# A recurrent attention block and its feed-forward part on one core: feed-forward groups of three chunks instead of two

## The chip, the cores and the metric

The kernel runs on 1 core of one Trainium2 chip. The metric is the device time of one execution in microseconds; three runs of the kernel before gave 1131.92, 1136.14 and 1138.54 us, median 1136.14 us. The profile is of one more execution.

## The reference, cut to what matters

```python
# r, k, v, w, a, b: (B=4, H=8, S=768, D=40) float32
for t in range(S):
    y[:, :, t] = np.einsum('bhd,bhde->bhe', rt, state)
    Sa = np.einsum('bhde,bhe->bhd', state, at)
    state = state * wt[:, :, None, :] - np.einsum('bhd,bhe->bhde', Sa, bt)
    state = state + np.einsum('bhd,bhe->bhde', vt, kt)
x = y.transpose(0, 2, 1, 3).reshape(3072, 320)     # tokens x (heads * D)
h = np.maximum(x @ w_in, 0.0)                       # w_in: 320 x 2048
out = (h * h) @ w_out                               # w_out: 2048 x 320
```

The two weight matrices arrive as float64, and the kernel rounds them to float32 itself.

## The kernel before, in words

**Chunks and slots.** The sequence is cut into chunks of 128 tokens; 6 chunks in each of 4 batches make 24 chunks, in the order of `order` (batch fastest). The main loop at the end (L766) has one slot for each chunk. A slot has `TOTAL` = 12 steps. In every step `weave` gives each of several generators its share of turns, so the order of the instructions on every engine is written out by this interleaving and each engine then runs its own list in order:

- `chain(i)`: the sequential part of chunk i on the matmul engine (PE): the product of A with v, two triangular solves with T (tiles `xr`, `minus_x`), the state's growth, and the outputs into `tokens` (L615).
- `rest(i+1)`: preparation of the next chunk: transposes (L315, `turn`), the masked products A and RV (L331), and at its end the loads of T and N (`inverses`).
- `prepare(i+...)`: the decays of later chunks (scans L354 and L355, reciprocals L358 and L359) in slots 0 to 15.
- `second`, the generator `ffn()`: the feed-forward part. A group is `GB` chunks. For each of the 16 tiles of 128 hidden units it does the first layer (contraction over 320 = two full tiles of rows with `w_in` and one of 64 rows with `w_third`), then relu on ScalarE (ACT, L642) and a multiplication on VectorE (DVE, L643), which squares; then it yields. Two tiles are started together, and the two `w_third` products of such a pair use the two halves of the array's rows. Then the second layer adds up 16 products of 320 columns for each chunk, with a yield after every 4.
- `rounded`, the generator `rounding()`: float64 weights to float32 in 26 pieces (10 of 512 columns for `w_in` and `w_third`, then 16 of 320 columns for `w_out`), each with two ACT and five DVE instructions (L257, L261, L265, L266, L274 to L276), through two tiles of `ps_f`.

**Queues.** Nearly all transfers are issued by SyncE (SP), in program order, each issue waiting for what it depends on. `store` puts a transfer into `line`, and a later `tick` issues it. When the last chunk of a group has its tokens, eight transfers (`moves`, from L620) gather rows of `tokens` into the 64-row tile and the spare rows; the first layer of the group waits for them, and `gathered` says when the generator may emit it. GpSimd (POOL) inverts triangular blocks in `solve`, after `take` has fetched them; after slots 0, 1, 3, 5, 9, 13 and 15 `flush`, `take` and `solve` stand between two slots.

**Where the feed-forward part stands.** Slots 0 to 3 contain none of it; they round 4, 7, 8 and 8 pieces. Before slot 4 the loop runs 8 feed-forward turns alone (`before` in L768 to L771). In slots 4 to 23 it has 12 turns a slot, one in every step. What is left runs after the last slot (`run(second)`). A group has 24 turns. All but the last group have two PSUM tiles (`ps_f`), the last has four (`ps_w`).

**Memory.** `hidden` holds 17 tiles of 256 columns, used in rotation; before the feed-forward part begins, float64 weights land in its first part and in two tiles `raw0` and `raw1`, five places for `w_out` in turn (`in_turn`), and its end serves as scratch for the first chunks (`spare`).

L87 is the line of the helper `mm`, so all products have that line; tiles tell them apart: `ps_c` belongs to the chain, `ps_w` to the preparation, `ps_f` to the feed-forward part and the rounding. Each product of float32 leaves two records in the trace (704 records of 352 products), each transpose one.

Of the kernel before, what the change touches and what calls it, by code (L numbers as in the profile page):

```python
# [17 lines left out]
def kernel(  # L18
# [25 lines left out]
    DM = H * D  # L44
# [7 lines left out]
    NF = DFF // 128  # L52
    GB = 2

# [34 lines left out]
    def single(name, shape):  # L89
        return const.tile(shape, FP32, tag=name, name=name)  # L90
# [141 lines left out]
    WIDE = len(fetches)  # L232
    in_turn = [*own_, *lent]
    for f in range(NF):
        fetchable(in_turn[f % 5], [(0, 128, moe_w_out[f * 128:(f + 1) * 128, :])], [w_out[:, f, :]])
# [101 lines left out]


    def spare(name, i):
        n = ("mv", "turned", "joins").index(name)  # L340
        t_ = hidden[:, NF - 2 * n - i % 2] if i <= B else own_[n // 2][:, n % 2 * H * Q:(n % 2 + 1) * H * Q]
        return t_.rearrange("p (h t) -> p h t", h=H)

# [148 lines left out]
    def rest(i, g):  # L492
# [16 lines left out]
        yield  # L509
        g["A"] = masked("A", 4, kT, aT)  # L510
        yield
# [115 lines left out]
    def ffn():  # L627
        for gi in range(len(order) // GB):
# [4 lines left out]
            for f in range(0, NF, 2):  # L633
# [4 lines left out]
                for e, p_ in enumerate(ps):  # L638
                    for j in range(NT):
                        mm(p_, w_in[:, j, (f + e) * 128:(f + e + 1) * 128], t_[:, j, :], False)  # L640
                    h_ = hidden[:, (gi * NF + f + e) % (NF + 1)]
                    nc.scalar.activation(h_, p_, Act.Relu)  # L642
                    nc.vector.tensor_tensor(h_, p_, h_, Alu.mult)  # L643
                    hid.append(h_)
                    yield True
            while left():
                yield False
            for n in range(GB):
                bb, c = order[gi * GB + n]
                p_ = psum(ps_f if gi < len(order) // GB - 1 else ps_w)[:, :DM]  # L650
                for f in range(NF):
                    mm(p_, hid[f][:, n * C:(n + 1) * C], w_out[:, f], f == 0)
                    if f % PART == PART - 1 and f < NF - 1:
                        yield True
                o_ = new("o", [128, DM], 1)
                nc.scalar.copy(o_, p_)
# [7 lines left out]
    gathered = set()  # L664
    STEPS = NF + 4 * GB

# [91 lines left out]

    TOTAL = STEPS // GB
    ahead = {0: (4, 5), 1: (6, 7), 2: (8,), 3: (9,), 4: (10, 11), 5: (12, 13)}  # L760
    ahead.update({i: (i + 8,) for i in range(6, len(order) - 8)})
    share = {**{i: (0, 0) for i in range(B)}, B: (TOTAL, 8)}
    pieces_in = {0: 4, 1: 7, 2: 8, 3: 8}
    done = set(range(B))
    unit = unit_of[B]
    for i in range(len(order)):  # L766
        bb, c = order[i]
        n, before = share.get(i, (TOTAL, 0))  # L768
        for _ in range(before):
            next(second)  # L770
            tick()  # L771
        tc.no_sync_barrier()
# [52 lines left out]
```

## Time and profile before

| what | value |
|---|---|
| median of the three runs | 1136.14 us |
| the profiled execution, its own time | 1136.86 us |
| its span, first to last instruction | 1135.1 us |
| mean granted TensorE clock | 0.908 |
| PE busy | 1029.9 us (91%) |
| DVE busy | 482.1 us (42%) |
| ACT busy | 246.2 us (22%) |
| POOL busy | 651.7 us (57%) |
| DMA | 113.48 MB, mean 100 GB/s |

1.8 us of the profiled execution lie outside its span. A row of the timeline gives the start in us, the duration in us, the engine, the line, the operation, the tiles, how many records were merged, and in brackets how long the engine sat idle before and what released it. PEld is the loading of the stationary operand.

### The profile page before, as it was taken

The numbers are of one execution on the slowest core, as the hardware profiler recorded it, in microseconds if no ns is written. First come the engines' busy times: TensorE is split into PE (matmuls) and PEld (weight loads), VectorE is DVE, ScalarE is ACT, GpSimd is POOL, SyncE is SP. The second block draws the span as 40 slices with busy tenths as digits, with TensorE's granted clock in tenths as the row PEclk, the third lists the DMA queues.
The fourth block names the chain that finished last, engine by engine and source line by source line (L and its number), as shares of the span: only waits on it lengthen the run. The fifth ranks groups of instructions, "written<-read, shape, count | busy, mean of one in ns | idle before, by whom it ended". The sixth has DMA issues, their size and how long they took to land.

```text
span 1135.1 us, 19336 instructions
## 1 busy us (share of the span) xinstructions
PE 1029.9 (91%) x7632; PEld 811.9 (72%) x7632; DVE 482.1 (42%) x1004; ACT 246.2 (22%) x547; POOL 651.7 (57%) x1129
## 2 busy tenths in 40 slices
PE   6385787799999999999999999999999999999998
PEld 5375676668777777777777777777777777777666
DVE  6367877727355155154264253353143133330211
ACT  2123233222221122122112122113021121221111
POOL 5886628877874999603999802999858810000000
PEclk8666656689999999999989999999998999999999
DMA  9889977583648505519515518414243342030000
GB/s 116 154 151 210 182 177 178 124 154 77 135 106 156 121 36 109 152 39 167 116 48 101 123 65 150 118 49 84 58 117 69 77 90 58 10 83 12 7 12 12
DMA packets 262370, 113.48 MB, mean 100 GB/s; under 512 B 244168, under 2 KB 250440, under 8 KB 260616
## 3 DMA queue, kind: packets, MB, share of 16 engines
q1 hardware_dynamic: 257944, 93.24, 40.2%
q0 software_dynamic: 3248, 18.88, 7.0%
q8 instruction: 60, 0.98, 0.4%
q10 hardware_dynamic: 1088, 0.13, 0.2%
q14 instruction: 30, 0.25, 0.1%
HBM read 75.77 MB, written 34.48 MB: 97 GB/s over the span
## 4 chain that ended last, share of the span: by engine, by line
PE 69%; DVE 11%; DMA 10%; SPq 3%; POOL 2%; issue 2%; ACT 2%; DVEq 0%; POOLq 0%; ACTq 0%
PE ps_f L87 34%; PE ps_c L87 19%; PE ps_w L87 11%; PE ps_w L315 3%; DMA in_v<-in_v_dram 3%; DVE decay L358 1%; DVE decay L359 1%; PE ps_w L533 1%; SPq L108 1%; DMA in_r<-in_r_dram 1%; DMA blocks<-kept_t 1%; POOL half_t L435 1%; POOL half_p L433 1%; DMA in_w<-in_w_dram 1%; PE ps_c L543 1%
## 5 line engine op out<-in xcount | busy, mean ns | idle before, releaser
L433 POOL TENSOR_TENSOR half_p<-half_n,half_t 128x70 f32<-128x70 f32 (+52 forms) x502 | 288.5, 575 | 104.9 <-DMA half_n<-kept_d 55.4
L435 POOL TENSOR_TENSOR half_t<-half_t,half_p 128x70 f32<-128x70 f32 (+52 forms) x502 | 315.2, 628 | 39.3
L643 DVE TENSOR_TENSOR hid<-ps_f,hid 128x256 f32<-128x256 f32 x176 | 73.9, 420 | 350.3 <-ACT hid L642 349.9
L87 PE MATMUL ps_f<-w_out,hid 128*128 128x320 f32 x704 | 208.2, 444 | 0.1
L87 PE MATMUL ps_f<-tokens,w_in 128*128 128x256 f32 x704 | 199.5, 410 | 0.0
L87 PEld LDWEIGHTS ps_f<-w_out,hid 128*128 128x128 f32 x704 | 130.4, 193 | 49.5 <-issue 2.4
L87 PEld LDWEIGHTS ps_f<-tokens,w_in 128*128 128x128 f32 x704 | 124.6, 196 | 43.5 <-issue 30.3
L642 ACT ACTIVATE hid<-ps_f 128x256 f32<-128x256 f32 x176 | 67.4, 383 | 269.1 <-PE ps_f L87 268.6
L87 PE MATMUL ps_f<-tokens,w_third 64*128 64x256 f32 x352 | 86.0, 425 | 8.1 <-DVE hid L643 6.0
L87 PEld LDWEIGHTS ps_c<-xr,T 64*64 64x64 f32 x768 | 54.9, 150 | 23.6 <-issue 13.8
L87 PE MATMUL ps_c<-xr,T 64*64 64x40 f32 x768 | 60.7, 241 | 7.2 <-DMA T<-kept_t 2.4
L410 POOL DMA_DIRECT2D half_n<-kept_d x18 | 8.9, 501 | 98.0 <-DMA kept_d<-N 92.9
L87 PEld LDWEIGHTS ps_f<-tokens,w_third 64*128 64x128 f32 x352 | 40.0, 190 | 34.9 <-DVE hid L643 23.0
L354 DVE TENSOR_TENSOR_SCAN decay<-ps_w,ones 128x64 f32<-128x64 f32 x88 | 23.6, 268 | 85.1 <-PE ps_w L315 85.1
L87 PEld LDWEIGHTS ps_c<-in_v,A 128*128 128x128 f32 x384 | 51.2, 209 | 2.3
L87 PE MATMUL ps_c<-in_v,A 128*128 128x40 f32 x384 | 50.2, 294 | 0.0
L87 PE MATMUL ps_w<-rT,xnT 40*128 40x128 f32 x384 | 36.4, 309 | 12.6 <-DVE RV L331 12.1
L87 PEld LDWEIGHTS ps_w<-rT,xnT 40*128 40x128 f32 x384 | 29.9, 206 | 22.9 <-DVE RV L331 18.9
L615 DVE TENSOR_TENSOR tokens<-ps_c,dec 128x512 f32<-128x512 f32 x24 | 16.5, 688 | 66.1 <-PE ps_c L87 66.1
L545 ACT COPY sd<-ps_c 128x512 f32<-128x512 f32 x20 | 11.7, 586 | 144.8 <-PE ps_c L543 144.8
L87 PE MATMUL ps_w<-decay,bT 40*128 40x128 f32 x352 | 28.4, 307 | 14.6 <-DVE decay L363 14.6
L370 ACT COPY N<-ps_w 128x512 f32<-128x512 f32 x48 | 25.8, 589 | 63.8 <-PE ps_w L87 44.2
(148 smaller groups left out, 1441.8 us busy)
## 6 DMA issues: line engine op xcount, KB each, us to landing
kept_e<-decay SPq DMA_DIRECT2D x22, 780.0 KB
dec<-kept_e SPq DMA_DIRECT2D x22, 780.0 KB
half_n<-kept_d POOLq DMA_DIRECT2D x12, 384.0 KB, 9.4
half_n<-kept_d POOLq DMA_DIRECT2D x6, 768.0 KB, 11.5
in_w<-in_w_dram SPq DMA_DIRECT2D x24, 160.0 KB
in_ab<-in_b_dram SPq DMA_DIRECT2D x24, 160.0 KB
in_ab<-in_a_dram SPq DMA_DIRECT2D x24, 160.0 KB
in_k<-in_k_dram SPq DMA_DIRECT2D x24, 160.0 KB
```

The costliest lines, as they stand in the source:

```text
L87: nc.tensor.matmul(o, l_, r_, start=start, stop=True, skip_group_check=True)
L108: later(lambda: queue.dma_start(out=out_, in_=in_), steps)
L315: nc.tensor.transpose(p_[:, q * 128:(q + 1) * 128], pair(x_, q), ident)
L354: nc.vector.tensor_tensor_scan(up[:, q, MID + 1:C + 1], wT[:, q, MID:], ones, 1.0, Alu.mult, Alu.mult)
L358: nc.vector.reciprocal(down[:, :, MID + 1:C + 1], up[:, :, MID + 1:C + 1])
L370: nc.scalar.copy(t_[:, e * NP:(e + 1) * NP], p_)
L433: nc.gpsimd.tensor_tensor(p_, part[:, at:at + m_].unsqueeze(1).to_broadcast([128, n, m_]), t3[:, :n, s:s + 1].to_broadcast([128, n, m_]), ...
L435: nc.gpsimd.tensor_tensor(t3[:, :n, s + 1:], t3[:, :n, s + 1:], p_, Alu.subtract)
L545: nc.scalar.copy(sd.rearrange("p q e d -> p q (e d)"), quads(p_))
L615: nc.vector.tensor_tensor(t_, y_, g["up"][:, :, :C], Alu.mult)
L642: nc.scalar.activation(h_, p_, Act.Relu)
L643: nc.vector.tensor_tensor(h_, p_, h_, Alu.mult)
```

## The change

`GB` becomes 3: a group is three chunks, the first layer's products have 384 columns instead of 256, there are 8 groups instead of 12, and a group has 28 turns. In slot 4 the feed-forward part has 8 turns from step 4 on, in slots 5 to 23 it has 10 turns in 12 steps (none in steps 0 and 6); the 8 turns alone before slot 4 are gone. The pieces rounded in slots 0 to 4 are 4, 6, 6, 7 and 4 (the last four within the first four steps of slot 4). `hidden` has 16 tiles of 384 columns without rotation; the tiles `raw0` and `raw1` are gone, and `w_out` has seven places in `hidden` instead of five. A has two tiles instead of four, `in_r` and `minus_x` one each instead of two, the output tile `o` two instead of one.

```diff
-    GB = 2
+    GB = 3
...
-            rings[nm] = Ring(f"in_{nm}", 2, [128, H, DP], 0.0, pads)
+            rings[nm] = Ring(f"in_{nm}", 1 if nm == "r" else 2, [128, H, DP], 0.0, pads)
...
-    minus_x = Ring("minus_x", 2, [128, H, DP], 0.0, pads)
+    minus_x = Ring("minus_x", 1, [128, H, DP], 0.0, pads)
...
-    hidden = single("hid", [128, NF + 1, GB * C])
+    hidden = single("hid", [128, NF, GB * C])
...
-    lent = [free_words[:, 2 * DM * i:2 * DM * (i + 1)] for i in range(3)]
-    own_ = [single(f"raw{i}", [128, 2 * DM]) for i in range(2)]
+    in_turn = [free_words[:, at:at + 2 * DM] for at in [4 * WI + 2 * DM * i for i in range(4)] + [2 * DM * i for i in range(3)]]
+    LENT = len(in_turn)
...
-    then = {0: (WIDE,), 1: (3,), 2: (WIDE + 1,), 3: (4,), 5: (WIDE + 2, WIDE + 3), 6: (WIDE + 4,)}
-    then.update({NARROW + f: (WIDE + f + 5,) for f in range(NF - 5)})
+    then = {1: (3,), 2: (WIDE,), 3: (4,), 4: (WIDE + 1,), 5: (WIDE + 2,), 6: (WIDE + 3,), 7: (WIDE + 4,), 8: (WIDE + 5,),
+            9: (WIDE + 6,)}
+    then.update({NARROW + f: (WIDE + f + LENT,) for f in range(NF - LENT)})
...
-        g["A"] = masked("A", 4, kT, aT)
+        g["A"] = masked("A", 2, kT, aT)
...
-                    h_ = hidden[:, (gi * NF + f + e) % (NF + 1)]
+                    h_ = hidden[:, f + e]
...
-                o_ = new("o", [128, DM], 1)
+                o_ = new("o", [128, DM], 2)
...
-    TOTAL = STEPS // GB
+    TOTAL = 12
...
-    share = {**{i: (0, 0) for i in range(B)}, B: (TOTAL, 8)}
-    pieces_in = {0: 4, 1: 7, 2: 8, 3: 8}
+    share = {**{i: (0, 0) for i in range(B)}, B: (8, 4)}
+    pieces_in = {0: (4, TOTAL), 1: (6, TOTAL), 2: (6, TOTAL), 3: (7, TOTAL), B: (4, 4)}
...
-        n, before = share.get(i, (TOTAL, 0))
-        for _ in range(before):
-            next(second)
-            tick()
+        n, begin = share.get(i, (10, 0))
...
-        jobs.append((some(second, n), n, 0, TOTAL))
+        jobs.append((some(second, n), n, begin, TOTAL))
         if i in pieces_in:
-            jobs.append((some(rounded, 2 * pieces_in[i]), 2 * pieces_in[i], 0, TOTAL))
+            m_, end = pieces_in[i]
+            jobs.append((some(rounded, 2 * m_), 2 * m_, 0, end))
```

How this moves instructions is seen at three places. A row below is a run of like instructions on one engine, with the line, the operation, the tiles, the size and the count.

The first place is PE at the border of slots 3 and 4; `blocks,hid` is the last product of `rest(4)`, and `in_v,A` the first of `chain(4)`. Before:

```order
L87 MATMUL ps_w<-hid 32x32 x16
L87 MATMUL ps_w<-decay_131,bT 128x128 x8
L87 MATMUL ps_w<-blocks,hid 32x32 x16
L87 MATMUL ps_f<-tokens,w_third 128x256 x2
L87 MATMUL ps_f<-tokens,w_in 128x256 x4
L87 MATMUL ps_f<-tokens,w_third 128x256 x2
L87 MATMUL ps_f<-tokens,w_in 128x256 x4
```

The same place after the change:

```order
L87 MATMUL ps_w<-hid 32x32 x16
L87 MATMUL ps_w<-decay_129,bT 128x128 x8
L87 MATMUL ps_w<-blocks,hid 32x32 x16
L87 MATMUL ps_c<-in_v_116,A 128x40 x8
L87 MATMUL ps_c<-state_134,dec 128x80 x4
L316 MATMUL ps_w<-ident,in_w_74 128x128 x4
L87 MATMUL ps_c<-xr,T 64x40 x8
L87 MATMUL ps_c<-minus_x_132,N_2289 64x40 x8
L316 MATMUL ps_w<-ident,in_k_107 128x128 x4
L316 MATMUL ps_w<-ident,in_ab_78 128x128 x4
L316 MATMUL ps_w<-ident,in_ab_79 128x128 x4
L87 MATMUL ps_f<-tokens,w_third 128x384 x2
```

The block of first-layer products that stood between the slots is gone; the first one now comes after the chain's second solve with `minus_x`, in step 4 of slot 4.

The second place is PE at the end of the last slot; `RX,in_b` is the last product of the last chain. Before:

```order
L87 MATMUL ps_c<-RX,in_b_111 64x128 x8
L87 MATMUL ps_f<-tokens,w_in 128x256 x2
L87 MATMUL ps_f<-tokens,w_third 128x256 x2
L87 MATMUL ps_f<-tokens,w_in 128x256 x4
L87 MATMUL ps_f<-tokens,w_third 128x256 x2
L87 MATMUL ps_f<-tokens,w_in 128x256 x4
```

The same place after the change:

```order
L87 MATMUL ps_c<-RX,in_b_111 64x128 x8
L87 MATMUL ps_f<-w_out,hid 128x320 x4
L87 MATMUL ps_w<-tokens,w_third 128x384 x2
L87 MATMUL ps_w<-tokens,w_in 128x384 x4
L87 MATMUL ps_w<-tokens,w_third 128x384 x2
```

Before, the rest of the eleventh group stands between the last chain and the twelfth group, which needs that chain's tokens; now only one turn of the second layer (4 products) stands between them.

The third place is SP at the end of slot 9, where `flush` and `take` follow; T and N belong to chunk 10, and the loads behind them to chunk 11. Before:

```order
L108 DMA tokens<-tokens 24x256
L108 DMA tokens<-tokens 40x256
L449 DMA T<-kept_t_225 64x8x64 x2
L458 DMA N_4954<-kept_n_164 64x512
L108 DMA kept_d_216<-N 32x8x64
L108 DMA kept_d_216<-N 32x8x32
L108 DMA kept_d_216<-N 32x8x64
L108 DMA kept_d_216<-N 32x8x32
L108 DMA kept_n_171<-N 512x1x64
L142 DMA in_k_107<-in_k_dram 128x8x40
L152 DMA dec<-kept_e_189 128x1560
L142 DMA in_r_115<-in_r_dram 128x8x40
```

The same place after the change:

```order
L108 DMA out_dram<-o 128x320
L448 DMA T<-kept_t_219 64x8x64 x2
L457 DMA N_4799<-kept_n_158 64x512
L108 DMA kept_d_210<-N 32x8x64
L108 DMA kept_d_210<-N 32x8x32
L108 DMA kept_d_210<-N 32x8x64
L108 DMA kept_d_210<-N 32x8x32
L108 DMA kept_n_165<-N 512x1x64
L142 DMA in_k_107<-in_k_dram 128x8x40
L152 DMA dec<-kept_e_183 128x1560
L142 DMA in_r_114<-in_r_dram 128x8x40
```

Before, the eight gathers (the last two are shown) are issued ahead of T and of the loads; now no gather falls on the end of slot 9, since groups end with slots 2, 5, 8, 11, 14, 17, 20 and 23 instead of every odd one.

More of the change, by code (lines that the diff above doesn't have):

```diff
@@ L232 @@
     WIDE = len(fetches)
-    in_turn = [*own_, *lent]
     for f in range(NF):
-        fetchable(in_turn[f % 5], [(0, 128, moe_w_out[f * 128:(f + 1) * 128, :])], [w_out[:, f, :]])
-    then = {0: (WIDE,), 1: (3,), 2: (WIDE + 1,), 3: (4,), 5: (WIDE + 2, WIDE + 3), 6: (WIDE + 4,)}
-    then.update({NARROW + f: (WIDE + f + 5,) for f in range(NF - 5)})
+        fetchable(in_turn[f % LENT], [(0, 128, moe_w_out[f * 128:(f + 1) * 128, :])], [w_out[:, f, :]])
+    then = {1: (3,), 2: (WIDE,), 3: (4,), 4: (WIDE + 1,), 5: (WIDE + 2,), 6: (WIDE + 3,), 7: (WIDE + 4,), 8: (WIDE + 5,),
+            9: (WIDE + 6,)}
+    then.update({NARROW + f: (WIDE + f + LENT,) for f in range(NF - LENT)})
     finished = [0]
@@ L339, in spare @@
     def spare(name, i):
-        n = ("mv", "turned", "joins").index(name)
-        t_ = hidden[:, NF - 2 * n - i % 2] if i <= B else own_[n // 2][:, n % 2 * H * Q:(n % 2 + 1) * H * Q]
-        return t_.rearrange("p (h t) -> p h t", h=H)
+        at = NF * GB * C - (("mv", "turned", "joins").index(name) * 2 + i % 2 + 1) * H * Q
+        return free_words[:, at:at + H * Q].rearrange("p (h t) -> p h t", h=H)
     def early(i, g=None):
@@ L664 @@
     gathered = set()
-    STEPS = NF + 4 * GB
     def run(gen):
```

## The prediction

> **What bounds the kernel now.** I read the windows by stage first, then the timeline of PE inside the stages, then the waits. A window row gives the stretch, its length, busy time (and records) of PE, PEld, DVE, ACT and POOL, the mean granted clock of TensorE, the DMA share and GB/s. The rows are slots 0 to 3, the feed-forward turns alone, slots 5 to 22, and what follows the last slot:
>
> ```profile
> 92.00:231.00 139.00, 103.86 (x896) 92.67 (x896) 110.61 (x217) 46.23 (x98) 94.75 (x205) 0.61 0.77 172
> 231.00:251.00 20.00, 18.36 (x62) 11.77 (x62) 4.37 (x10) 4.21 (x12) 15.02 (x36) 0.83 0.98 169
> 294.00:1031.00 737.00, 710.11 (x5330) 555.48 (x5329) 279.32 (x588) 146.56 (x330) 443.32 (x603) 0.97 0.42 92
> 1059.00:1136.00 77.00, 71.53 (x284) 48.05 (x283) 11.45 (x27) 11.93 (x31) 0.00 (x0) 1.00 0.03 11
> ```
>
> From 294 us on PE is busy for 710 of 737 us, so there one microsecond of products less is nearly one less on the clock, and the feed-forward turns are PE's filler while the chain waits for its copies. In slots 0 to 3 DVE is the busiest (110.6 of 139) and the clock stands at 0.61.
>
> **The price of a turn.** The dense rows are those of the last group, where nothing else runs (a row gives start, duration):
>
> ```profile
> 1094.09 0.70 PE L87 MATMUL ps_w<-tokens,w_third 64*128 64x256 f32 x4
> 1094.72 1.99 PE L87 MATMUL ps_w<-tokens,w_in 128*128 128x256 f32 x8
> 1096.65 0.70 PE L87 MATMUL ps_w<-tokens,w_third 64*128 64x256 f32 x4
> 1097.82 0.81 PE L87 MATMUL ps_w<-tokens,w_in 128*128 128x256 f32 x3
> 1114.45 17.39 PE L87 MATMUL ps_w<-w_out,hid 128*128 128x320 f32 x64
> ```
>
> The view of the tile `tokens` gives these records' durations, least, median and most, in ns:
>
> ```profile
> L87 PE MATMUL ps_w<-tokens,w_in x64: 379/379/484, 1094.7 to 1114.2; 128*128 128x256 f32 x64
> ```
>
> Start to start, the two w_third products (four records) take 0.63 us and the eight w_in records 1.93, so a pair of hidden tiles costs 2.56, and eight pairs 20.5. Three w_in records of 0.379 end 0.81 after the first starts, so they start 0.216 apart. Eight make 1.73, so 0.20 is lost where w_in ends and the 64-row shape begins; w_third, two streams side by side of two records, is 0.43 and again 0.20. This loss belongs to the change of shape, not to the columns. At 384 columns a record is 0.324: w_third 0.65 + 0.20 = 0.85, w_in 2.59 + 0.20 = 2.79, a pair 3.64 for three chunks against 3.84 for the same in groups of two. The second layer stays at 17.39 / 64 = 0.272 a record, 8.7 us a chunk. Inside the slots a pair is split by other work:
>
> ```profile
> 255.56 0.70 PE L87 MATMUL ps_f<-tokens,w_third 64*128 64x256 f32 x4
> 256.19 1.13 PE L87 MATMUL ps_f<-tokens,w_in 128*128 128x256 f32 x4
> 257.25 1.12 PE L87 MATMUL ps_c<-minus_x,N 64*64 64x40 f32 x16
> 258.30 1.13 PE L87 MATMUL ps_f<-tokens,w_in 128*128 128x256 f32 x4
> 259.27 0.60 PE L315 MATMUL ps_w<-ident,in_k 128*128 128x128 f32 x4
> 260.67 0.70 PE L87 MATMUL ps_f<-tokens,w_third 64*128 64x256 f32 x4
> 273.83 2.42 PE L87 MATMUL ps_f<-w_out,hid 128*128 128x320 f32 x8
> 276.19 1.16 PE L87 MATMUL ps_w<-rT,xnT 40*128 40x128 f32 x16
> ```
>
> 0.63 + 1.06 + 0.97 is 2.66, hence about 1.31 to 1.33 a first-layer turn; I take 1.31 before and, with 0.22 more for w_third and 0.43 more for each w_in, 1.85 after. A second-layer turn is 2.36 here and 8.7 / 4 = 2.18 dense; I take 2.25.
>
> **The sum, term by term.** (1) The turns alone before slot 4 go:
>
> ```profile
> 229.58 1.09 PE L87 MATMUL ps_w<-blocks,hid 32*32 32x32 f32 x32
> 231.78 1.74 PE L87 MATMUL ps_f<-tokens,w_third 64*128 64x256 f32 x4 [1.11 <-DVE w_out L265]
> 240.86 0.70 PE L87 MATMUL ps_f<-tokens,w_third 64*128 64x256 f32 x2
> 250.47 1.87 PE L87 MATMUL ps_c<-in_v,A 128*128 128x40 f32 x16
> ```
>
> From 230.67 to 250.47 that is -19.8. Dense they would be 10.2; the first two pairs ran at the low clock (9.08 instead of 5.12), the others waited for two PSUM tiles to be emptied.
>
> (2) Slot 4 had 8 first-layer and 4 second-layer turns (19.5) and gets 8 of 1.85 (14.8): -4.7. But its first four steps have no filler and round one piece each, like slots 0 to 3, whose 48 steps took 139 us, 2.9 each: 11.6. Before, the same work took from 250.47 to 260.67, 10.2, with a w_third (0.63) and three w_in (1.06 and two of 0.97) in it, 6.6 without: +5.0. The low clock that met the turns alone (9.08 - 5.12 = 4.0) now falls into this slot. Together +4.3.
>
> (3) Slots 0 to 3 round three and a half narrow pieces fewer. Two DVE rows of the same instruction, one piece apart, and one ACT row:
>
> ```profile
> 188.65 0.47 DVE L265 SCALAR_TENSOR_TENSOR w_out<-raw,ps_f 128x320 int32<-128x320 int32 x1
> 191.15 0.49 DVE L265 SCALAR_TENSOR_TENSOR w_out<-hid,ps_f 128x320 int32<-128x320 int32 x1
> 172.60 0.50 ACT L261 ACTIVATE w_out<-raw 128x320 f32<-128x320 uint32 x1 [7.77 <-DMA raw<-in_moe_w_out_dram]
> ```
>
> A narrow piece keeps DVE for 2.5 us, three and a half for 8.8, and the chain of waits runs through these instructions over and over between 155 and 232 us. ACT's one long wait, 7.77 us for a weight transfer, should shrink with seven places. Bounds: 0 (other waits take over) to -13 (pieces and half the wait). I take -7.
>
> (4) Slots 5 to 22 have 180 turns, 104 of the first layer and 76 of the second, 192.4 + 171.0 = 363.4; before 216, 144 and 72, 188.6 + 162.0 = 350.6: +12.8. The slots carry more of the feed-forward part, because less stands outside them. Slot 23, without preparation, shows its first-layer turns waiting for PSUM:
>
> ```profile
> 1047.83 1.26 PE L87 MATMUL ps_f<-tokens,w_third 64*128 64x256 f32 x4
> ```
>
> 1.26 where 0.70 is the rule, in each of three pairs. Its five first-layer and three second-layer turns (6.6 + 6.8, and 1.7 of waits) become seven of the second layer (15.8): +0.7.
>
> (5) After the last chain:
>
> ```profile
> 1056.74 1.04 PE L87 MATMUL ps_c<-RX,in_b 128*64 128x128 f32 x16
> 1058.55 6.17 SPq L108 DMA_DIRECT2D tokens<-tokens  x8
> 683.52 1.78 DMA tokens<-tokens
> 1131.92 0.42 ACT L656 COPY o<-ps_w 128x320 f32<-128x320 f32 x1 [8.19 <-PE ps_w L87]
> ```
>
> From 1057.78 to the end are 77.3 us. Before, the rest of group 10 covered the gather. Now 2.2 us of second layer do: the eight issues end at 6.94 after the last chain product, and with a transfer of 1.8 to 2.2 the tokens are there at 9.0, so PE stands 6.8 us. Then 8 x 3.64 = 29.1, 26.1 for three chunks of the second layer, 3.3 from the last product to the end, and a cold clock (below) 5.1: 72.6, hence -4.7.
>
> (6) Waits inside slots 5 to 22. The first two rows are PE's waits for the mask of RV, over the whole span and in 90 to 232 us; the windows show the clock after the wait at 851.69:
>
> ```profile
> PE ps_w L87 <- DVE RV L331: 12.1, 7, 5.2
> PE ps_w L87 <- DVE RV L331: 6.0, 2, 5.2
> 533.04 0.66 PE L315 MATMUL ps_w<-ident,in_r 128*128 128x128 f32 x4 [2.69 <-DMA in_r<-in_r_dram]
> 851.69 1.61 PE L87 MATMUL ps_c<-xr,T 64*64 64x40 f32 x16 [1.74 <-DMA T<-kept_t]
> 848.00:852.00 4.00, 2.26 (x19) 1.83 (x18) 0.42 (x1) 0.80 (x2) 3.45 (x8) 1.00 0.52 125
> 852.00:856.00 4.00, 4.00 (x22) 2.82 (x20) 0.00 (x0) 0.42 (x1) 3.56 (x6) 0.50 1.11 282
> 856.00:860.00 4.00, 4.00 (x22) 3.18 (x21) 0.42 (x1) 0.80 (x2) 3.58 (x6) 0.50 1.38 161
> 860.00:864.00 4.00, 4.00 (x23) 2.56 (x22) 0.48 (x2) 0.77 (x2) 3.53 (x7) 0.72 0.04 7
> ```
>
> A wait of 1.74 us is followed by 4.0 x 0.50 + 4.0 x 0.50 + 4.0 x 0.28 = 5.1 us of lost clock: 6.8 an event. The five RV waits after 232 us (6.1 us) stand where DVE does two reciprocals while PE has two turns to fill with; those are now longer by up to 0.54 each, -3. The wait for in_r in slot 10 comes behind eight gathers on SP, which now end slots 8 and 11 instead of 9, and slot 14 likewise: -4. The gather ahead of T in slot 17 stays, and so I leave that event. Bounds: -14 (clock losses go too) to +5 (two steps of every slot have no filler).
>
> (7) Edits at no cost. A's two tiles are read by the chain in step 1 and written from step 6 on, on the same PE order; in_r is read in step 7 of the slot before its next load, later than in_k must wait anyway; minus_x is read to the end of step 7 and written in step 2 of the next slot. Relu and square grow with the columns, and 128 of them replace 192:
>
> ```profile
> L643 DVE TENSOR_TENSOR hid<-ps_f,hid 128x256 f32<-128x256 f32 x176 | 73.9, 420 | 350.3 <-ACT hid L642 349.9
> L642 ACT ACTIVATE hid<-ps_f 128x256 f32<-128x256 f32 x176 | 67.4, 383 | 269.1 <-PE ps_f L87 268.6
> ```
>
> Between these and one and a half times them, emptying a pair takes at most 0.4 us more, which the chain's products between two turns cover.
>
> Sum: -19.8 + 4.3 - 7 + 12.8 + 0.7 - 4.7 - 7 = -20.7. The profiled execution's own time is 1136.86, which gives 1116; it stands 0.7 above the median of the runs, so 1115.
>
> **A rule against the trace.** The Trainium skill, "TensorE: Matmul & The Clock Gate", Back-to-back issue gap, gives a matmul its columns over the clock and a fixed 2.5 ns, so wider products would win next to nothing. By it a first-layer turn is 1.5 x 1.31 = 1.97; the 0.20 at each change of shape is what the rule leaves out. The same page, The HAM clock gate, has the low clock come after an idle window of some 3.4 us and go after as long; the event at 851.69 disagrees on both (1.74 us of wait, over 8 us of low clock). By it the end would lose 1.7 instead of 5.1, and the sum would be 1112.
>
> **The rivals.**
> Columns alone: the product's cost is in proportion to columns, shape changes included. Then 104 turns x 0.12 and the last group's 16 x 0.10 add 14: 1129. For it: records of 256 and of 320 columns (0.216, 0.272) are in proportion; against it: the two gaps of 0.20 a pair.
> More waits vanish: with the mean clock 0.97 over 737 us, 22 us of clock are lost there; if half of it and term (3) at its bound come too, 1115 - 11 - 5 = 1099.
> Thin filler: steps 0 and 6 leave the chain's copies bare. At 0.8 us a slot (a copy and its handover) over 19 slots, +15: 1130, no change that can be measured. Against it: what stands in step 6 does not read step 5's copy without a turn between.
> Slower: each group's first product comes before its gathers have landed, as after the last slot. Groups now begin a step to a third of a slot after their last chunk; one event costs 6.8, and from four on the gain is gone; six give 1156. For it, group 6 begins in step 1 of slot 21. Against it, group 1 begins a slot late and groups 2 to 5 in step 3 of a slot or later, over 9 us after their tokens.
>
> **Chances.** Forecast 0.60 (1107 to 1122), more waits vanish 0.14, columns alone 0.08, thin filler 0.11, slower 0.07. The range 1100 to 1130 leaves out the slower case and about half of two others. A measurement of this kernel tells about 0.5% (5.7 us) from no change: faster 0.84 (the first two, columns alone, some of thin filler), same 0.10, slower 0.06.
>
> **What would show it.** In the profile after: no first-layer row between the last blocks product and in_v,A of slot 4; w_in rows of 384 columns 0.32 apart; slots 5 to 22 longer by some 0.3 us each; a wait of PE for a gather of 6 to 7 us after the last chain, then a clock near 0.5; no DMA wait of PE near the start of slots 10 and 14. The prediction is wrong if the slots grow by over 1 us each, or if slot 4 starts no earlier than 225 us.

## The result, and the profile after

| kernel | median | against the kernel before (95% interval) |
|---|---|---|
| before | 1134.03 us | 1 |
| after | 1093.77 us | 0.9644 (0.9595 to 0.9693) |

The change gains 40 us, twice what was predicted (1115), and the time lies outside the range (1100 to 1130). The profiled execution took 1096.7 us, with a span of 1095.0 against 1135.1. The windows of the kernel after, in the columns of the prediction's first fence, are slots 0 to 3 without their first 66 us, slot 4, slots 5 to 22, and what follows the last chain product:

```profile
92.00:232.00 140.00, 102.41 (x891) 92.17 (x891) 97.75 (x195) 41.15 (x86) 95.75 (x207) 0.60 0.79 170
232.00:282.00 50.00, 48.18 (x381) 35.60 (x378) 34.63 (x73) 16.71 (x36) 33.23 (x78) 0.80 0.77 145
282.00:998.00 716.00, 703.12 (x5120) 515.07 (x5121) 275.26 (x549) 143.26 (x292) 457.30 (x623) 0.99 0.45 95
1025.00:1095.00 70.00, 61.91 (x204) 35.37 (x200) 9.62 (x17) 9.57 (x20) 0.00 (x0) 0.93 0.04 13
```

DVE has 13 us less to do in the first row, and yet the row isn't shorter. In slots 5 to 22 PE is idle for 13 us (before 27), and the mean granted clock is 0.99 (before 0.97). PE's waits in these slots, first those of before (294 to 1031 us; the last, 0.6 us, left out), then all of those of after (282 to 998 us), as total, times and longest:

```profile
PE ps_w L87 <- DVE RV L331: 6.1, 5, 1.7
PE ps_w L533 <- DVE RX L331: 5.4, 10, 0.6
PE ps_f L87 <- DVE hid L643: 4.2, 12, 0.8
PE ps_w L315 <- DMA in_r<-in_r_dram: 3.6, 2, 2.7
PE ps_w L315 <- DMA in_v<-in_v_dram: 2.6, 2, 2.1
PE ps_c L87 <- DMA T<-kept_t: 2.4, 3, 1.7
PE ps_c L87 <- ACT hid L642: 1.0, 1, 1.0
...
```

```profile
PE ps_w L532 <- DVE RX L332: 6.6, 10, 0.8
PE ps_w L87 <- DVE RV L332: 3.8, 3, 1.9
PE ps_f L87 <- DVE hid L642: 1.1, 3, 0.5
PE ps_c L87 <- DMA T<-kept_t: 1.0, 1, 1.0
```

The waits for transfers fell from 8.6 us to 1.0, those for hid from 5.2 to 1.1, those for RV from 6.1 to 3.8. The start of slot 4 and the end, in rows of PE and SP (SPq marks the issuing of transfers by SP):

```profile
231.25 1.09 PE L87 MATMUL ps_w<-blocks,hid 32*32 32x32 f32 x32
232.28 1.98 PE L87 MATMUL ps_c<-in_v,A 128*128 128x40 f32 x16
244.77 2.17 PE L87 MATMUL ps_f<-tokens,w_third 64*128 64x384 f32 x4 [1.31 <-DVE w_out L266]
1025.14 2.42 PE L87 MATMUL ps_f<-w_out,hid 128*128 128x320 f32 x8
1025.97 6.25 SPq L108 DMA_DIRECT2D tokens<-tokens  x8
1032.41 2.98 PE L87 MATMUL ps_w<-tokens,w_third 64*128 64x384 f32 x4 [4.85 <-DMA tokens<-tokens]
...
1040.49 0.92 PE L87 MATMUL ps_w<-tokens,w_third 64*128 64x384 f32 x4
1041.33 2.85 PE L87 MATMUL ps_w<-tokens,w_in 128*128 128x384 f32 x8
1044.11 0.92 PE L87 MATMUL ps_w<-tokens,w_third 64*128 64x384 f32 x4
```

The turns alone are gone, and a pair at full clock takes 3.62 us start to start. The first pair of the last group takes 8.08, so 4.5 us are lost behind a wait of 4.85 us.

Put together from the starts of the slots (first row `in_v,A` of each), with differences taken before rounding:

| stretch | before | after | measured | predicted |
|---|---|---|---|---|
| slots 0 to 3, to the end of `rest(4)` | to 230.7 | to 232.3 | +1.6 | -7 |
| turns alone | 19.8 | 0 | -19.8 | -19.8 |
| slot 4 | 43.7 | 49.6 | +5.9 | +4.3 |
| slots 5 to 22 | 737.0 | 716.3 | -20.7 | +5.8 (+12.8 - 7) |
| slot 23, to the last chain product | 26.5 | 27.0 | +0.4 | +0.7 |
| the end | 77.4 | 69.9 | -7.5 | -4.7 |
| sum | | | -40.1 | -20.7 |

Two rows are wrong: the first, and slots 5 to 22. The latter I split into PE's idle time, clock not granted (each window of 4 us times one minus its clock), and the rest, products at full clock. Idle fell from 27.0 to 12.9, lost clock from 20.5 to 6.8, and the products grew from 689.5 to 696.6. These figures come from one profiled execution of each kernel; five other executions of kernels that have the same slots 5 to 22 took 713.1 to 716.2 us there, with products of 696.2 to 698.2.

### The profile page after: what moved, and what is told of

Its sections match the earlier page's. It is cut to its first block, busy times and chain, and to the rows that moved or that the text cites. A ratio compares the mean times of both kernels' runs of the same rounds, so it can differ in the third digit from the quotient of the medians.

```text
span 1095.0 us, 18413 instructions
## 1 busy us (share of the span) xinstructions
PE 996.7 (91%) x7248; PEld 746.5 (68%) x7248; DVE 470.3 (43%) x940; ACT 236.1 (22%) x483; POOL 653.2 (60%) x1127
## 4 chain that ended last, share of the span: by engine, by line
PE 75%; DVE 9%; DMA 8%; POOL 3%; SPq 2%; issue 2%; ACT 1%; DVEq 0%; POOLq 0%; ACTq 0%
PE ps_f L87 35%; PE ps_c L87 19%; PE ps_w L87 13%; PE ps_w L316 4%; PE ps_w L532 1%; DMA half_n<-kept_d 1%; POOL half_p L432 1%; DMA dec<-kept_e 1%; DMA blocks<-kept_t 1%; POOL half_t L434 1%; SPq L108 1%; DVE decay L357 1%; DVE decay L358 1%; PE ps_c L542 1%; PE ps_c L585 1%
## 5 line engine op out<-in xcount | busy, mean ns | idle before, releaser
L87 PE MATMUL ps_f<-w_out,hid 128*128 128x320 f32 x672 | 199.5, 442 | 0.0
L87 PE MATMUL ps_f<-tokens,w_in 128*128 128x384 f32 x448 | 174.6, 514 | 0.0
L642 DVE TENSOR_TENSOR hid<-ps_f,hid 128x384 f32<-128x384 f32 x112 | 61.8, 552 | 232.2 <-ACT hid L641 232.1
L87 PEld LDWEIGHTS ps_f<-w_out,hid 128*128 128x128 f32 x672 | 122.6, 192 | 44.4 <-issue 1.4
L87 PEld LDWEIGHTS ps_f<-tokens,w_in 128*128 128x128 f32 x448 | 78.0, 193 | 63.9 <-issue 33.2
L641 ACT ACTIVATE hid<-ps_f 128x384 f32<-128x384 f32 x112 | 55.0, 491 | 217.4 <-PE ps_f L87 217.4
L87 PEld LDWEIGHTS ps_c<-xr,T 64*64 64x64 f32 x768 | 55.4, 151 | 25.7 <-issue 22.1
L87 PE MATMUL ps_f<-tokens,w_third 64*128 64x384 f32 x224 | 62.2, 536 | 2.4 <-DVE w_out L266 1.3
L332 DVE TENSOR_TENSOR A<-ps_w,upper 128x512 f32<-128x512 f32 x48 | 30.9, 685 | 48.3 <-PE ps_w L87 48.3
L87 PE MATMUL ps_c<-in_v,A 128*128 128x40 f32 x384 | 49.6, 292 | 0.0
L332 DVE TENSOR_TENSOR RX<-ps_w,upper 128x512 f32<-128x512 f32 x48 | 30.8, 684 | 39.9 <-PE ps_w L87 39.8
L87 PE MATMUL ps_w<-decay,bT 40*128 40x128 f32 x352 | 28.5, 308 | 17.9 <-DVE decay L362 15.6
L503 DVE TENSOR_TENSOR kvT<-ps_w,dec 128x512 f32<-128x512 f32 x24 | 16.4, 683 | 61.3 <-PE ps_w L316 36.6
L87 PEld LDWEIGHTS ps_w<-rT,xnT 40*128 40x128 f32 x384 | 27.8, 202 | 19.9 <-DVE RV L332 14.0
## 6 DMA issues: line engine op xcount, KB each, us to landing
half_n<-kept_d POOLq DMA_DIRECT2D x12, 384.0 KB, 10.2
```

Of the source, the lines that this page charges most:

```text
L87: nc.tensor.matmul(o, l_, r_, start=start, stop=True, skip_group_check=True)
L332: nc.vector.tensor_tensor(t_, p_, over4(upper), Alu.mult)
L503: nc.vector.tensor_tensor(kT, kT_, down[:, :, 1:C + 1], Alu.mult)
```

## The experiments

Times are medians, ratios are against the kernel before, which ran beside each set.

**The layout alone, in groups of three.** The early layout was put back into the kernel after:

```diff
-    share = {**{i: (0, 0) for i in range(B)}, B: (8, 4)}
-    pieces_in = {0: (4, TOTAL), 1: (6, TOTAL), 2: (6, TOTAL), 3: (7, TOTAL), B: (4, 4)}
+    share = {**{i: (0, 0) for i in range(B)}, B: (4, 4)}
+    pieces_in = {0: (4, TOTAL), 1: (7, TOTAL), 2: (8, TOTAL), 3: (8, TOTAL)}
...
+        for _ in range(8 if i == B else 0):
+            next(second)
+            tick()
```

> Groups of three as in the changed kernel, but the early layout of the kernel before: pieces 4, 7, 8, 8 in slots 0 to 3, eight turns alone ahead of slot 4, four more in slot 4. If the prediction's terms (1) to (3) hold, the layout is worth 19.8 - 4.3 + 7 = 22.5 us and this takes 1116. If slots 0 to 3 gain nothing from fewer pieces, as the two traces say (230.7 against 232.3), it is worth about 12 and this takes 1106. If the layout is also what shortened slots 5 to 22 (by 20.8), it takes over 1120.

Measured: 1124.7 us, 0.9925 (0.989 to 0.996). Slot 5 begins 11.0 us later than in the kernel after, slots 5 to 15 take 6.8 less (idle and lost clock alone, the products take 443.3 in both), and slots 16 to 22 take 22.5 more. Those 22.5 are a fault of my edit, and the rival "slower" of the prediction seen at work. Rows of PE:

```profile
826.67 3.06 PE L87 MATMUL ps_f<-tokens,w_third 64*128 64x384 f32 x4 [3.50 <-DMA tokens<-tokens]
939.36 0.88 PE L87 MATMUL ps_f<-tokens,w_third 64*128 64x384 f32 x2 [4.06 <-DMA tokens<-tokens]
```

Twelve turns up to slot 4 instead of eight put the feed-forward part four turns ahead, and later groups then begin before their tokens are gathered. The second try took one turn out of each of slots 5 to 8 (`n, begin = share.get(i, (9 if i < 9 else 10, 0))`).

> The early layout with groups of three again, with nine turns a slot instead of ten in slots 5 to 8, so that from slot 9 on as many turns have been made as in the changed kernel (the first run was four turns ahead of it, and PE waited for tokens three times, 8.1 us, with 18.8 us of low clock in slots 16 to 22). If those waits, and not the layout, made the rest of the first run's loss, the slots from 9 on are as in the changed kernel; slot 5 begins 11 us later and four turns of 1.85 less stand in slots 5 to 8: 1094 + 11 - 7 = 1098. If the early layout itself costs what the first run showed, it stays at 1120 or above.

Measured: 1111.0 us, 0.9762 (0.9724 to 0.98). Slots 16 to 22 take 254.4, as after (254.3), and no wait for tokens is left, so the distance of a group from its last chunk was the cause. The time lies between the two cases expected. Slot 5 begins 12.6 us later than in the kernel after, and slots 5 to 8, with four turns fewer, give nothing of that back: they take 173.8, where after took 173.7. Nine turns in twelve steps leave steps 0, 4 and 8 empty, and PE now waits up to 4.2 us for RV there. I had looked only at how many turns a slot has; where they stand had to be looked at too.

**The layout alone, in groups of two.** The kernel before with the late layout (pieces 4, 6, 6, 7 and 4, eight turns from step 4 of slot 4, thirteen a slot in slots 5 to 16; tokens held three times, A two tiles instead of four).

> Groups of two as in the kernel before, but the late layout: pieces 4, 6, 6, 7 and 4 in slot 4, no turns alone, eight turns from step 4 of slot 4 on; the twelve turns taken out there are put into slots 5 to 16, thirteen a slot (tokens held three times and A once, for room). If the layout is a gain by itself, it takes 1134 - 12 = 1122 or less. If the gain of the layout exists only because groups of three leave fewer turns to place, the twelve turns cost their price again in the slots (12 x 1.31 to 2.25, about 20): 1134 - 19.8 + 1.6 + 1.9 + 20 = 1138. The waits in slots 5 to 15 should stay near 24 us of idle and 15 us of clock if they hang on the groups, and fall if more filler is enough.

Measured: 1127.8 us, 0.9916 (0.9881 to 0.9951), between the two cases. Slots 0 to 3 are 5.1 us shorter than before beside the 19.8 of the turns alone, which speaks for term (3) in groups of two; but it is one execution, and the starts of slot 4 in four executions with the early part of the kernel before lie 4.7 us apart. Slots 5 to 22 take 13.9 more for twelve turns more, with 27.1 us of idle and 17.0 of lost clock: more filler by itself took no wait away.

**Slots 1 to 3.** DVE waits for dec in the kernel after. The first two rows are those waits, in slots 2 and 3; the next are SP's issues ahead of the first, and around the second:

```profile
168.13 0.69 DVE L503 TENSOR_TENSOR kvT<-ps_w,dec 128x512 f32<-128x512 f32 x1 [8.37 <-DMA dec<-kept_e]
207.91 0.69 DVE L503 TENSOR_TENSOR kvT<-ps_w,dec 128x512 f32<-128x512 f32 x1 [5.23 <-DMA dec<-kept_e]
140.45 1.20 SPq L249 DMA_DIRECT2D hid<-in_moe_w_out_dram  x2
152.01 0.63 SPq L249 DMA_DIRECT2D hid<-in_moe_w_out_dram  x1
153.17 0.61 SPq L152 DMA_DIRECT2D dec<-kept_e  x1
189.97 6.78 SPq L108 DMA_DIRECT2D tokens<-tokens  x8
200.96 0.66 SPq L152 DMA_DIRECT2D dec<-kept_e  x1
```

In slot 2 dec is used 15 us after its issue, behind three weight transfers of 320 KB. In slot 3 the issue itself is late, behind the first group's eight moves. Three kernels tried this. The first delays each weight transfer by two more steps:

```diff
-                    later(lambda m_=m_: fetch_weights(m_, nc.sync), 1)
+                    later(lambda m_=m_: fetch_weights(m_, nc.sync), 3)
```

> The changed kernel, with each weight transfer put on SP's queue three steps after its piece instead of one, so that those of a slot's last steps stand behind the next slot's in_k, dec and in_r. If loads are the next bound of slots 1 to 3 (waits of PE for in_k 10.4 us and of DVE for dec 15.7 us), these slots lose 4 to 8 us and the run takes 1086 to 1090. If the loads are late for want of transfer rate (DMA share 0.96 in slot 1) or if something else binds, the change is under 2 us.

Measured: 1091.0 us, 0.9617 (0.9582 to 0.9653), not to be told from after; slot 4 begins at 232.4. `flush`, after slot 1, empties `line` whatever the delay, so ahead of slot 2 the order stayed as it was: an edit that missed its place. The second fetches five pieces ahead in place of seven:

```diff
-    then = {1: (3,), 2: (WIDE,), 3: (4,), 4: (WIDE + 1,), 5: (WIDE + 2,), 6: (WIDE + 3,), 7: (WIDE + 4,), 8: (WIDE + 5,),
-            9: (WIDE + 6,)}
-    then.update({NARROW + f: (WIDE + f + LENT,) for f in range(NF - LENT)})
+    then = {1: (3,), 3: (4, WIDE), 4: (WIDE + 1,), 5: (WIDE + 2,), 7: (WIDE + 3,), 9: (WIDE + 4,)}
+    then.update({NARROW + f: (WIDE + f + 5,) for f in range(NF - 5)})
```

> The changed kernel, with the last weights' transfers five ahead of their piece instead of seven (places and pieces as they were). In slot 2, dec lands 15 us after its issue, against 6 in the run with the late layout and groups of two, where two transfers of 320 KB fewer had been asked for by then. If the deeper prefetch takes the transfer rate from in_k and dec, slots 1 to 3 lose 3 to 6 us and slot 4 begins at 227 to 229 instead of 232: 1088 to 1091. If not, ACT waits for the weights instead, and it is 1094 or more.

Measured: 1085.8 us, 0.9549 (0.9506 to 0.9592). Slot 2 takes 39.2 us instead of 43.8, and the wait of 8.37 is gone; that of slot 3 is still there, at 2.88:

```profile
152.94 0.62 SPq L152 DMA_DIRECT2D dec<-kept_e  x1
...
160.68 5.92 SPq L250 DMA_DIRECT2D hid<-in_moe_w_out_dram  x1
...
202.23 0.69 DVE L504 TENSOR_TENSOR kvT<-ps_w,dec 128x512 f32<-128x512 f32 x1 [2.88 <-DMA dec<-kept_e]
```

In the eight profiles of groups of three with transfers seven deep DVE waits 5.5 to 8.5 us for dec in slot 2, in the four with five deep not at all. The third kernel, told below with the end, holds the first group's moves until the middle of slot 3.

**The moves, added to the kernel after.** `flush` stands after slots 5, 9, 13 and 15. In groups of two the eight moves come after every second slot, 1, 3, 5 and so on, so at each of these places they go ahead of in_k, dec and in_r of the next slot. In groups of three they come after slots 2, 5, 8 and so on, and meet only the one after slot 5. Eight idle moves, of half the size and to a tile that nobody reads, were put after chunks 9 and 13:

```diff
+        if i in (9, 13):
+            for j, row, h, d, m_ in moves:
+                at = (h % 2) * DP + d
+                store(nowhere[row:row + m_], t_[at:at + m_, h // 2], 1)
```

> The changed kernel, with eight more moves (of half the size, to a tile that nobody reads) on SP after chunks 9 and 13, where the kernel before had its gathers and waited for in_r and in_v in slots 10 and 14. If the moves on SP made those waits, PE waits there again, 2 to 3.5 us a slot with 1.7 to 2.6 us of low clock behind each: 8 to 12 us, so 1102 to 1106. If the waits came from the solver's transfers alone, it stays within 1.5 us of 1094.

Measured: 1095.0 us, 0.966 (0.9624 to 0.9696). The waits come back in slots 10 and 14, but as 3.4 us in all (T, dec, in_v, in_r, each 0.3 to 1.1), and these slots grow by 4.3 us together, without lost clock beyond that of after. The direction is that of the theory, the size less than half, and the time by itself is the one expected if the moves do not matter (within 1.5 us of 1094). The kernel after also has a meeting of its own, after chunk 5: there in_k is issued 6.5 us into slot 6 (4.5 in the kernel before), and yet PE waits for no transfer in slot 6, where the kernel before waited 2.09 us for in_v. So in groups of three a late load costs less; why is not shown.

**The place of the turns.** The kernel after with the empty steps at 3 and 9, and then at 0 and 4, in place of 0 and 6:

```diff
+    def but(gen, empty):
+        for step in range(TOTAL):
+            if step not in empty:
+                next(gen, None)
+            yield
...
-        jobs.append((some(second, n), n, begin, TOTAL))
+        jobs.append((but(second, (3, 9)), TOTAL, 0, TOTAL) if n == 10 else (some(second, n), n, begin, TOTAL))
```

> The changed kernel, with the two steps of a slot that hold no turn put at steps 3 and 9 instead of 0 and 6 (ten turns in twelve steps as before). If it matters that steps 0 and 6 are bare (the thin-filler rival at 0.8 us a slot) or that they are the right ones, the 18 slots change by 0.5 us each or more: 9 us either way. If any ten of twelve steps do, it stays within 3 us of 1094.

Measured: 1114.2 us, 0.9791 (0.9743 to 0.9838), some two fifths of the change's gain lost by moving two empty steps in every slot. Then steps 0 and 4:

> The changed kernel with steps 0 and 4 empty instead of 0 and 6. With steps 3 and 9 empty it took 20 us more. If that came from step 9, next to the mask of RV and the reciprocals, and from a turn in step 0 ahead of the chain, this one is within 4 us of 1094. If six steps between two empty ones is what matters, it is 1100 or more.

Measured: 1085.1 us, 0.9547 (0.9492 to 0.9602): a gain over the kernel after, though the two intervals just touch. The windows of slots 5 to 15 and 16 to 22, of the first run, of after, and of the second:

```profile
278.40:751.00 472.60, 457.35 (x3293) 334.36 (x3292) 199.32 (x393) 91.43 (x186) 345.81 (x437) 0.98 0.51 106
751.00:1012.30 261.30, 257.89 (x1831) 185.22 (x1829) 76.12 (x155) 51.01 (x105) 110.79 (x187) 0.99 0.33 69
```

```profile
281.90:743.90 462.00, 450.08 (x3295) 331.07 (x3294) 198.52 (x393) 91.84 (x187) 340.75 (x432) 0.99 0.52 108
743.90:998.20 254.30, 253.34 (x1829) 184.25 (x1828) 76.83 (x156) 51.41 (x105) 116.65 (x192) 1.00 0.34 71
```

```profile
280.60:736.70 456.10, 445.37 (x3296) 329.69 (x3294) 196.83 (x393) 91.68 (x187) 336.22 (x428) 0.99 0.53 110
736.70:990.10 253.40, 252.26 (x1830) 183.71 (x1829) 78.25 (x156) 51.02 (x105) 120.31 (x196) 1.00 0.34 72
```

With 5,124 to 5,126 records PE is busy for 715, 703 and 698 us, and idle for 19, 13 and 12; of the busy time 12, 7 and 5 are lost clock. In the first run, whose step 0 is filled, group 6 also begins before its tokens (two waits, 2.5 us).

**Place and moves in the kernel before.** The place alone, without changing the groups: twelve turns with none in steps 0 and 6 and two each in 8 and 9 (the helper `turns` makes as many turns in each step as its list says).

```diff
-        jobs.append((some(second, n), n, 0, TOTAL))
+        jobs.append((turns(second, (0, 1, 1, 1, 1, 1, 0, 1, 2, 2, 1, 1)), TOTAL, 0, TOTAL) if n else (some(second, n), n, 0, TOTAL))
```

> The kernel before, groups of two, with its twelve turns a slot put as the changed kernel puts its ten: none in steps 0 and 6, two each in steps 8 and 9, where DVE makes its reciprocals and the mask of RV. If the place of the turns is what took the waits out of slots 5 to 22 (12.3 us less idle in 5 to 15, 13.7 less of low clock in 5 to 22), the kernel before gains most of that: 1134 - 15 to 20 = 1114 to 1119. If the groups did it (fewer gathers, fewer changes between the layers, wider products), only RV's waits shrink (6.1 us) and those for in_r, in_v, T and hid stay: 1128 to 1136.

Measured: 1132.5 us, 0.9995 (0.9957 to 1.0034). PE's waits from 280 to 1010 us, the longer ones:

```profile
PE ps_c L87 <- DMA T<-kept_t: 11.9, 4, 3.1
...
PE ps_w L87 <- DVE kvT L504: 4.9, 1, 4.9
PE ps_w L315 <- DMA in_k<-in_k_dram: 4.2, 1, 4.2
PE ps_f L87 <- DVE hid L643: 2.2, 4, 0.7
PE ps_w L87 <- DVE RV L331: 2.1, 3, 0.8
```

RV's waits fell from 6.1 to 2.1 us and those for hid from 4.2 to 2.2; PE is earlier at T, dec (through kvT) and in_k, which stand behind the moves on SP, and loses it all there. To test this, the moves after chunks 5, 9 and 13 were given to POOL, alone and then with this place:

```diff
-                store(t_[row:row + m_, j], t_[at:at + m_, h // 2], 1)
+                store(t_[row:row + m_, j], t_[at:at + m_, h // 2], 1, nc.gpsimd if i in (5, 9, 13) else nc.sync)
```

> The kernel before, with the eight moves after chunks 5, 9 and 13 issued by POOL, which is idle there, instead of SP, whose queue holds T, in_k, dec and in_r of the next slot behind them. If the moves on SP made the waits for transfers in slots 6, 10 and 14 (6.5 us, and up to 8 us of low clock after them), these waits go: 1134 - 6 to - 14 = 1120 to 1128. If the solver's transfers, which start in the same place, make them, it stays within 2 us of 1134.

> The kernel before with both: the turns in the changed kernel's steps (none in 0 and 6, two in 8 and 9) and the moves after chunks 5, 9 and 13 issued by POOL. The place alone gave nothing, since waits for T, in_k and dec (18 us more) took the place of those for RV and hid. If those come from the moves on SP, they go in slots 6, 10 and 14, and slots 8 and 18 keep theirs: 1134 - 12 to - 20 = 1114 to 1122. If the loads are late for the solver's transfers or because the slots are shorter, it stays at 1128 or above.

Measured: alone 1128.5 us, 0.9922 (0.9888 to 0.9955); both 1111.2 us, 0.9771 (0.9738 to 0.9804). In the first, no wait for a transfer is left in slots 6, 10 and 14, and these three take 7.4 us less. The second takes 27.2 us less in these three than the kernel with the place alone, and the other slots together as much as there. SP's and POOL's rows of the first at the start of slot 10 (507.4):

```profile
...
507.46 0.57 SPq L142 DMA_DIRECT2D in_k<-in_k_dram  x1
508.13 0.59 SPq L152 DMA_DIRECT2D dec<-kept_e  x1
501.49 3.60 POOL L108 DMA_DIRECT2D tokens<-tokens  x7 [23.21 <-DVE tokens L615]
```

In the kernel before, this slot began at 511.5, its eight moves stood on SP until 511.5, and in_k was issued at 516.7. The stretches of slots 5 to 22, from starts and windows as above:

| kernel, groups of two | slots 5 to 22 | idle | lost clock | products at full clock |
|---|---|---|---|---|
| before | 737.0 | 27.0 | 20.5 | 689.5 |
| place | 737.9 | 35.7 | 25.6 | 676.6 |
| moves | 725.3 | 19.3 | 15.3 | 690.7 |
| both | 711.3 | 20.0 | 11.9 | 679.4 |

The place row's execution took 1138.75 us, 6.3 above that kernel's median, so this row is rather high. Neither half is worth much alone, and together they take 25.7 us from these slots without any change of the groups, where the change took 20.7. But 15.6 of the 25.7 are idle and lost clock, and the change took 27.8 of these. In the kernel with both, PE still waits 6.9 us for T in slots 8, 18 and 22, behind gathers that were left on SP; groups of three have no gather ahead of slots 8 and 22. No run took those away alone.

**The end, and what adds up.** Three runs worked on the wait after the last chain. The last group's eight moves on three queues by turns:

```diff
+            queues = [nc.sync, nc.scalar, nc.gpsimd] if i == len(order) - 1 else [nc.sync]
```

> The changed kernel, with the eight moves of the last group issued by three queues (SP, ACT, POOL by turns) instead of SP alone. If the eight issues in a row (6.25 us) are what PE waits for after the last chain, they end some 4 us sooner, the wait falls from 4.85 us to about 1, and the low clock behind it (4.5 us) goes with it: 1085 to 1088. If the clock stays low all the same, 1090. If issues on ACT and POOL are slower or start later, no change.

Measured: 1091.4 us, 0.9584 (0.9542 to 0.9626), not to be told from after. The wait fell only to 3.6 us, in two parts: ACT's issues stand behind its copy of `o`, and begin 1.9 us after SP's. Next, on top of the transfers five deep, five of the eight moves by POOL and three by SP, and slot 23 with eight turns instead of ten.

> The run with transfers five deep (1085.8), with two turns of slot 23 kept for after the last chain, and the last group's moves issued by POOL (five) and SP (three). If the tail's wait (4.85 us) and the low clock behind it (4.5) are the gather's eight issues in a row and nothing else, both go and slot 23 gives its two turns back at their price: 1077 to 1079. If ACT's copy ahead of its issues was not what held the three-queue run to 3 us, the wait stays at 2 us or more and the clock low: 1082 to 1085.

Measured: 1082.0 us, 0.9527 (0.9481 to 0.9572). PE's wait and the product behind it:

```profile
1020.70 0.91 PE L87 MATMUL ps_w<-tokens,w_third 64*128 64x384 f32 x2 [1.66 <-DMA tokens<-tokens]
1021.53 2.85 PE L87 MATMUL ps_w<-tokens,w_in 128*128 128x384 f32 x8
```

The wait is 1.66, and the clock stays full. Then the first group's moves were held until the middle of slot 3, and in the last run the empty steps put at 0 and 4 as well.

> The same, with the first group's eight moves held back from the end of slot 2 until step 5 of slot 3, behind that slot's in_k, dec and T. If the moves ahead of dec (6.8 us of SP's queue) are what DVE waits for in slot 3 (5.2 us), slot 3 loses 2 to 5 us against the run without. If the transfers are limited by rate, it is the same within 1.5 us.

> The changed kernel with transfers five deep, the first group's moves held, the tail's moves on two queues with two turns kept for it, and the empty steps at 0 and 4: the runs measured 1078.1 for all but the last, and the last alone took 8.7 us from the changed kernel. If they add up, 1069 to 1073. If the gain of the empty steps was mostly a clock that happened to be granted, 1075 to 1079.

Measured: 1078.1 us, 0.9496 (0.9452 to 0.954), slot 3 at 37.8 us instead of 41.1; and 1074.8 us, 0.9458 (0.9419 to 0.9498). The last is 2% faster than the kernel after. The gains do not add up in full: the empty steps, worth 8.7 us alone, bring 3.3 here, with intervals that overlap, and the time lies between the two cases expected.

## Why the prediction was wrong, point by point

**Term (6), the waits in slots 5 to 22: the step that failed.** It allowed 7 us, of bounds -14 to +5; idle and lost clock fell by 27.8, half of it clock, and the slots shrank by some 1.2 us each instead of growing by 0.3. The prediction had itself measured that a wait can cost several times its length in clock, and then left the clock out of the sum. Its rival "more waits vanish" (1099, with a chance of 0.14) had the clock about right, 11 us for 13.7, but its time came near by luck, since it also wanted term (3) at its bound, which did not come. The event that the prediction left in the sum as staying, 1.74 us of wait for T behind the gather that ends slot 17, and 5.1 of clock after it, was gone for the most part, though the gather still stands there. In the kernel after:

```profile
824.50 1.09 PE L87 MATMUL ps_c<-xr,T 64*64 64x40 f32 x16 [0.96 <-DMA T<-kept_t]
```

No clock was lost behind this one, so the event alone makes 5.9 of the 27.8.

Two causes are shown, in groups of two, where together they take 15.6 of idle and lost clock. The moves of every second chunk meet the solver's boundary each time and hold up the next slot's loads; the prediction saw this for in_r in two slots, at 4 us. Taken out alone they were worth 11.7 us of slots 5 to 22, 7.4 of it in the three slots concerned (6, 10 and 14); idle and lost clock fell by 12.9. And the place of the turns, which the prediction treated as a possible loss ("thin filler", +15), is a gain of 14.0 us once the loads are not late, 11.3 of it in the products and 2.7 in idle and clock. In groups of three the place bears on the waits too: with the empty steps at 3 and 9 idle and lost clock are 10.9 us more. The other 12.2 us of the 27.8 stay open. Fewer gathers ahead of T, as told above, would fit for slots 8 and 22 but not for slot 18; what the 384 columns themselves hide would fit too: the eight moves put back into the kernel after cost 4.3 us in two slots, less than their removal gave in the kernel before. Neither was tested by itself.

**Term (4), the filler: sign right, size off.** Predicted +12.8, products at full clock measured +7.1. The place of the turns may have taken part of it back: in groups of two, products of the same number and kind took 11.3 us less with the turns placed so. With groups of three this was not measured apart.

**Term (3), slots 0 to 3: no gain where 7 us were forecast.** DVE had 12.9 us less to do in the first window, more than the 8.8 counted on. The step that failed is that a freed DVE would be followed by shorter slots: dec was late next, since the seven places, which I took for a gain to ACT, also ask for weights sooner, and the first group's moves now stand ahead of slot 3's loads. In five executions with this early part slot 4 begins at 229.4 to 235.0, so the +1.6 is no loss that can be told; but the sign that the prediction named against itself, a slot 4 that starts no earlier than 225, came true. With weights fetched five pieces ahead and the moves held, slot 4 begins at 224.0, and in the last run at 223.5, instead of 232.3.

**Right.** The turns alone (-19.8), slot 23, the price of a pair (3.62 for 3.64), no wait for a transfer at slots 10 and 14. Slot 4 took +5.9 for +4.3, and the low clock did fall into it (10.2 us lost); that the size fits is partly luck, since in seven of eight other runs with the same slot 4 it took 45.6 us, which is +1.9, with 6.8 lost. The claim that the slots do not wait for groups held, but with fewer than four turns to spare, as the first experiment showed. "Columns alone" is excluded by the pair's price, which it puts at 3.84.

**The end.** -7.5 for -4.7: a wait of 4.85 for 6.8. The issues took 6.25 (6.17 before), but PE started 0.2 us after the last one, not 1.8 to 2.2. The low clock cost 4.5 where I had taken 5.1. The Trainium skill, "TensorE: Matmul & The Clock Gate", The HAM clock gate, has low clock after an idle window of some 3.4 us, in a window that runs freely. Here 4.85 us brought it and 1.66 did not, which agrees; the 1.74 us of the kernel before, and 1.79 in the last run below, did bring it, and 1.78 in the run with the moves held did not, so the length alone does not decide. The loss behind the 4.85 was 4.5, not the 1.7 that the prediction worked out from that rule.

## What to carry to other kernels

Price a wait with the clock that it costs, and put that into the sum, not into a rival. Where filler stands between the steps of a chain can matter as much as how much of it there is, but only if what comes next on the path (here loads behind a queue) isn't late by then: one half-measure was worth nothing that can be measured, the other 0.8%, and both together 2.3%. When an engine is relieved, find in the profile which transfer it will wait for next, and what has been put ahead of that on its queue; and a prefetch that goes deeper can delay a load that is due sooner.

## What the runs showed of the hardware

Products of the same number and kind do not take the same time on PE in another order. In slots 5 to 22 the kernel with the moves on POOL has 690.7 us of them at full clock, and with the place changed too 679.4. In slots 16 to 22 alone, both with a clock of 0.99, the two are:

```profile
764.50:1021.40 256.90, 254.17 (x1914) 198.87 (x1913) 77.43 (x169) 51.99 (x119) 115.02 (x191) 0.99 0.33 72
750.50:1002.90 252.40, 248.28 (x1913) 196.76 (x1912) 76.89 (x170) 52.38 (x120) 120.38 (x196) 0.99 0.33 72
```

PE is busy for 5.9 us less, 0.8 a slot, while its idle time rises from 2.7 to 4.1. Some 0.7 of this is the mix, an estimate from the prediction's prices, as in these slots the first kernel has one turn of the second layer more and one of the first layer less. The cause is not settled: changes from one kind of product to the next fall only from 226 to 217, which at the prediction's 0.20 us each would be some 2 us, an estimate.

POOL issues a move in 0.51 us (seven in 3.60), SP in 0.78 (eight in 6.24), and POOL's are not behind the loads.

The clock after a wait is not settled by the wait's length. In the last run a wait of 1.79 us, in the place of the 1.66 above, is followed by a low clock:

```profile
1011.02 0.91 PE L87 MATMUL ps_w<-tokens,w_third 64*128 64x384 f32 x2 [1.79 <-DMA tokens<-tokens]
1011.86 4.50 PE L87 MATMUL ps_w<-tokens,w_in 128*128 128x384 f32 x8
```
